# Attention with memory slots and a three-way maxout FFN: weights by column thirds, batch 1's sums in two parts, a new order of work

## The chip, the cores and the metric

The kernel runs on one core of one Trainium2 chip. The metric is the device time of a launch in microseconds (us), the median of several runs. A profile shows the same program from its first to its last instruction; that span is about 2 us shorter than the time. Work is spread over TensorE (matmul; PE in the profile), VectorE (DVE), ScalarE (ACT), GpSimd (POOL, here mostly the issuer of loads) and SyncE (SP, which issues the stores).

## The reference

Eight batches, eight heads, 576 positions, head size 64, and 32 memory slots per head; then a feed-forward block over all 4608 tokens of width 512, with an inner width of 768.

```python
a   = softmax(phi, axis=2)                      # [b, h, s, 32]
k_m = einsum('bhsm,bhsd->bhmd', a, k)           # 32 summed keys per head
v_m = einsum('bhsm,bhsd->bhmd', a, v)
attn = softmax(q @ k_m.T / sqrt(64), axis=-1)   # [b, h, s, 32]
x   = (attn @ v_m) rearranged to [4608, 512]
h   = maximum(maximum(x @ w1, x @ w2), x @ w3)  # [4608, 768]
out = h @ w_out                                 # [4608, 512], fp32
```

The kernel never forms `x`. It multiplies the summed values of a batch into the weights ("folds" them), so that the FFN works on the attention weights directly. It also uses max(a, b, c) = c + max(a - c, b - c, 0): w3 is subtracted from w1 and w2, and w3 @ w_out is computed once and folded too.

## The kernel before: the parts that matter

All matmul operands are bf16, sums are fp32 in PSUM. One pool of four PSUM buffers (two banks each) serves every matmul group.

```python
acc_pool = ctx.enter_context(tc.tile_pool(name="accp", bufs=4, space=bass.MemoryType.PSUM))
ctx.enter_context(tc.manual_schedule())         # engines keep the order of the text below
# loads; all but phi of batch 0 are issued by GpSimd, with a cast from fp32 to bf16 (phi: none)
load_ph(0); load_kv(0); load_q(0)               # load_kv(0): k and v in halves
load_w(2)                                       # w3, one transfer
nc.gpsimd.dma_start(out=wo_sb, in_=...)         # w_out
make_identity(nc, ident)
load_w(0); load_w(1)                            # w1, w2, one transfer each
load_ph(1); load_kv(1); load_q(1)               # load_kv: k, then v
# ... cut ...
EVAC = {"D": "avaa", "T": "vavav"}              # which engine drains: a ScalarE, v VectorE
```

Each step has a letter. `W@0` is the step W of batch 0.

```python
Z  warm_up(n)      n matmuls 128x512 on zeros (fill time on TensorE, results unused)
E  att_exp         e = exp(phi)                                   ScalarE
B  att_kv          72 small matmuls: e^T [k | v | 1] -> kvp       (the 1s give the sum of e)
N  att_kv_norm     1/sum, v part * 1/sum, k part * 1/sum          VectorE
K  att_kv_t        3 transposes of the normalised parts           VectorE drains
Q  att_q(n)        transpose of half of q                         VectorE
S  att_score       32 small matmuls, then two exps                ScalarE
M  att_sum(g)      sum over the slots by a matmul with ones
R  att_rec(g)      r = exp(-ln(sum)), two operations              ScalarE
X  att_mul(g)      attn = e2 * r                                  VectorE
W  w3_t(f2)        8 transposes of w3                             VectorE drains
O  w3_o(j)         6 matmuls: w3 @ w_out, a quarter               ScalarE drains
V  w_diff(n)       w1 - w3, w2 - w3, in three parts               VectorE
D  fold(b, n)      8 small matmuls 64x512; n = 3 folds w3 @ w_out; one PSUM buffer, drained to wp
F  ffn1(b, n)      4 matmuls 128x288; tile n // 2 of the inner width, n % 2 = 0 for w1, 1 for w2
T  ffn2(b, t)      6 + 2 matmuls 128x512, drained to SBUF and stored by SyncE
L  loads: L0 phi, L1 k and v, L2 q
```

```python
def w_diff(n):                                  # n-th 512 columns of [w1 | w2], 1536 wide
    c = n * BANK
    while c < (n + 1) * BANK:
        e = min((n + 1) * BANK, (c // DF + 1) * DF)
        nc.vector.tensor_tensor(out=w12[:, :, c:e], in0=w12[:, :, c:e],
                                in1=w_sb[:, :, 2, c % DF : c % DF + e - c], op=ALU.subtract)
        c = e

def ffn1(b, n):
    ft, w = n // 2, n % 2
    # ... lhsT = wps[b][:, g, w * DF + ft * P : w * DF + (ft + 1) * P] ...
    if w == 0:
        nc.scalar.activation(out=h1, in_=a, func=AF.Relu)                    # max(a - c, 0)
    else:
        nc.vector.tensor_tensor(out=hT[...], in0=a, in1=s["h1", ft], op=ALU.max)
```

The order of the first part, as it stands in the text of before:

```python
E@0 Z26@0 B@0 N@0 Z5@0 K@0 Q0@0 Q1@0 Z8@0 S@0 Z8@0 W1@0 W2@0 M0@0 W0@0 L0@2 R0@0
Z9@0 O2@0 M1@0 V0@0 X0@0 R1@0 O0@0 X1@0 V2@0 O3@0 L1@2 Z3@0 D0@0 O1@0 F6@0 F0@0 F2@0
D2@0 F4@0 V1@0 D3@0 D1@0 F7@0 F5@0 F10@0 F11@0 F1@0 E@1 F3@0 F8@0 F9@0 B@1 N@1 Q0@1
T3@0 K@1 Q1@1 T1@0 S@1 D1@1 L2@2 D0@1 M0@1 M1@1 R1@1 R0@1 X1@1 T0@0 X0@1 T2@0 E@2
...
```

A step's place in this text sets its place in each engine's own queue; across engines only the data, the buffers and the transfers hold it back.

Of the kernel before, what the change touches and what calls it, by code (L numbers as in the profile page):

```python
# [8 lines left out]
FP32 = mybir.dt.float32  # L9
BF16 = mybir.dt.bfloat16  # L10
AF = mybir.ActivationFunctionType
ALU = mybir.AluOpType
# [3 lines left out]
def kernel(  # L16
# [12 lines left out]
    nc = tc.nc  # L29
# [13 lines left out]
    BANK = 512  # L43

# [3 lines left out]
    quad = ctx.enter_context(tc.tile_pool(name="quad", bufs=4))  # L48
    opool = ctx.enter_context(tc.tile_pool(name="opool", bufs=6))
# [41 lines left out]
    def load_kv(b):  # L91
        kv = kvos[b % 2]
        loaded.setdefault(b, {})["kv"] = kv
        for h in halves if b == 0 else [slice(0, NP)]:
            for i, src in enumerate((k, v)):
                nc.gpsimd.dma_start(  # L96
                    out=kv[:, i].rearrange("p j c d -> p j (c d)")[:, h],
                    in_=by_pair(src, b)[:, h],
                )
# [8 lines left out]
    def load_w(i):  # L108
        w = (moe_w1, moe_w2, moe_w3)[i]
        nc.gpsimd.dma_start(  # L110
            out=w_sb[:, :, i], in_=w.rearrange("(j p) f -> p j f", p=P)
        )

    load_ph(0)
    load_kv(0)
    load_q(0)
    load_w(2)
    nc.gpsimd.dma_start(out=wo_sb, in_=moe_w_out.rearrange("(t p) c -> p t c", p=P))
    ident = const.tile([P, P], BF16, name="ident")
    make_identity(nc, ident)  # L120
    load_w(0)
    load_w(1)
    load_ph(1)
    load_kv(1)
    load_q(1)

# [18 lines left out]
    EVAC = {"D": "avaa", "T": "vavav"}  # L145

    def evacuate(kind, n, out_, in_):
        e = EVAC[kind][n]
        if e == "s":
            nc.scalar.copy(out=out_[:, 0], in_=in_[:, 0])  # L150
            nc.vector.tensor_copy(out=out_[:, 1], in_=in_[:, 1])
        elif e == "a":
            nc.scalar.copy(out=out_, in_=in_)  # L153
        else:
            nc.vector.tensor_copy(out=out_, in_=in_)  # L155


    def w3_t(f2):

        pt = acc_pool.tile([P, 2, NP, P], BF16, name="pt", tag="acc")  # L160
        for i in range(2):
            f = 2 * f2 + i
            for j in range(NP):
                nc.tensor.transpose(
                    pt[:, i, j, :], w_sb[:, j, 2, f * P : (f + 1) * P], ident
                )
        nc.vector.tensor_copy(out=w3T[:, 2 * f2 : 2 * f2 + 2], in_=pt)

    def w3_o(j):
        po = acc_pool.tile([P, DM], FP32, name="po", tag="acc")  # L170
        for f in range(FT):
            nc.tensor.matmul(
                po,
                lhsT=w3T[:, f, j, :],
                rhs=wo_sb[:, f, :],
                start=(f == 0),
                stop=(f == FT - 1),
            )
        nc.scalar.copy(out=w3o[:, j, :], in_=po)

    w12 = w_sb[:, :, 0:2].rearrange("p j i f -> p j (i f)")

    def w_diff(n):

        c = n * BANK
        while c < (n + 1) * BANK:
            e = min((n + 1) * BANK, (c // DF + 1) * DF)
            nc.vector.tensor_tensor(
                out=w12[:, :, c:e],
                in0=w12[:, :, c:e],  # L190
                in1=w_sb[:, :, 2, c % DF : c % DF + e - c],
                op=ALU.subtract,
            )
            c = e

# [9 lines left out]
    def att_kv(b, js=range(NP)):  # L207
        s = st[b]
        if "kvp" not in s:
            s["kvp"] = acc_pool.tile([P, NG, BANK], FP32, name="kvp", tag="acc")  # L210
        kv, kvp = loaded[b]["kv"], s["kvp"]
        for c in range(NC):
            for j in js:
                for a in range(NG):
                    r = slice(HP * a, HP * (a + 1))
                    nc.tensor.matmul(  # L216
                        kvp[M * j : M * (j + 1), a, 0 : 3 * D],
                        lhsT=s["e"][r, j, c, :],
                        rhs=kv[r, :, j, c, :],
                        start=(c == 0),  # L220
                        stop=(c == NC - 1),
                        tile_position=(HP * a, M * j),
                    )

    def att_kv_norm(b):

        s = st[b]
        kvp = s["kvp"]
        rden = work.tile([P, NG], FP32, name="rden")
        nc.vector.reciprocal(out=rden, in_=kvp[:, :, 2 * D])  # L230
        kvn = work.tile([P, 3, P], BF16, name="kvn")
        nc.vector.tensor_tensor(
            out=kvn[:, 0].rearrange("p (a d) -> p a d", a=NG),
            in0=kvp[:, :, D : 2 * D],
            in1=rden.unsqueeze(2).to_broadcast([P, NG, D]),
            op=ALU.mult,
        )
# [10 lines left out]
        s["kvn"] = kvn  # L248

    def att_kv_t(b):  # L250


        s = st[b]
        ps = acc_pool.tile([P, 3, P], BF16, name="kvtp", tag="acc")
        for n in range(3):
            nc.tensor.transpose(ps[:, n], s["kvn"][:, n], ident)  # L256
        kvt = work.tile([P, 3, P], BF16, name="kvt")
        nc.vector.tensor_copy(out=kvt, in_=ps)
        s["kvt"] = kvt
# [84 lines left out]
    def fold(b, n):  # L344
# [7 lines left out]
        for j in range(NP):  # L352
            for a in range(NG):
# [4 lines left out]
                    rhs=w12[r, j, n * BANK : (n + 1) * BANK] if n < 3 else w3o[r, j, :],  # L358
# [5 lines left out]
            "D", n, wp3s[b] if n == 3 else wps[b][:, :, n * BANK : (n + 1) * BANK], ps  # L364
# [5 lines left out]
    def ffn1(b, n):  # L370
# [4 lines left out]
        hT, attn = hts[b // 2], attns[b // 2]  # L375
        acc = acc_pool.tile([P, 2, BANK], FP32, name="acc", tag="acc")
        for g in range(NG):
            for h in range(2):
# [3 lines left out]
                    lhsT=wps[b][:, g, w * DF + ft * P : w * DF + (ft + 1) * P],  # L382
# [5 lines left out]
        if w == 0:  # L388
            h1 = s["h1", ft] = quad.tile([P, 2, SH], BF16, name="h1")
            nc.scalar.activation(out=h1, in_=a, func=AF.Relu)  # L390
# [10 lines left out]
    def ffn2(b, t, last=False):  # L401
# [4 lines left out]
        if last:  # L406
            return ffn2_last(b, c0)
# [31 lines left out]
        evacuate("T", t, ot, po)  # L439
# [34 lines left out]
    def first_kv():  # L474
        for n, h in enumerate(halves):
            att_kv(0, range(NP)[h])
            if n == 0:
                warm_up(9)


    def issue(b, n):

        if not 0 <= b < B or (n == "T4" and b % 2 == 0):
            return
        i = int(n[1:]) if len(n) > 1 else None
        {
            "L": lambda: (load_ph, load_kv, load_q)[i](b),
            "E": lambda: [att_exp(b, h) for h in (halves if b == 0 else [slice(0, NP)])],
            "B": lambda: att_kv(b) if b else first_kv(),
            "N": lambda: att_kv_norm(b),  # L490
            "K": lambda: att_kv_t(b),
# [5 lines left out]
            "D": lambda: fold(b, i),  # L497
            "F": lambda: ffn1(b, i),
            "T": lambda: ffn2(b, i),
            "W": lambda: w3_t(i),  # L500
            "O": lambda: w3_o(i),
# [4 lines left out]
    def run(b, text):  # L506

        for w in text.split():
            issue(b + w.count("+") - w.count("-"), w.rstrip("+-"))

    for w in """
        E@0 Z26@0 B@0 N@0 Z5@0 K@0 Q0@0 Q1@0 Z8@0 S@0 Z8@0 W1@0 W2@0 M0@0 W0@0 L0@2 R0@0
        Z9@0 O2@0 M1@0 V0@0 X0@0 R1@0 O0@0 X1@0 V2@0 O3@0 L1@2 Z3@0 D0@0 O1@0 F6@0 F0@0 F2@0
        D2@0 F4@0 V1@0 D3@0 D1@0 F7@0 F5@0 F10@0 F11@0 F1@0 E@1 F3@0 F8@0 F9@0 B@1 N@1 Q0@1
        T3@0 K@1 Q1@1 T1@0 S@1 D1@1 L2@2 D0@1 M0@1 M1@1 R1@1 R0@1 X1@1 T0@0 X0@1 T2@0 E@2
        D3@1 F2@1 F0@1 F3@1 D2@1 B@2 N@2 F1@1 Q1@2 F8@1 Q0@2 L0@3 F6@1 F4@1 L1@3 F10@1 K@2
        F7@1 F5@1 L2@3 S@2 F11@1 D2@2 F9@1 E@3 M0@2 T2@1 M1@2 R0@2 R1@2 X0@2 L0@4 T0@1 D0@2
        X1@2 D3@2 B@3 N@3 D1@2 L1@4 T1@1 F2@2 F6@2 Q1@3 F3@2 E@4 K@3 F8@2 L2@4 F7@2 L0@6
        Q0@3 F4@2 F10@2 F5@2 F0@2 S@3 L0@5 T4@1 M1@3 F11@2 R1@3 F1@2 M0@3 R0@3 X0@3 T3@1
        F9@2 D2@3 D1@3 L2@5 X1@3 B@4 D0@3 T1@2 F8@3 L1@5 N@4 F2@3 K@4 F9@3 Q1@4 F10@3 F0@3  # L520
        E@5 F3@3 Q0@4 F4@3 T3@2 S@4 F5@3 F1@3 L1@6 T0@2 F6@3 M0@4 M1@4 F11@3 R0@4 T2@2 R1@4
        F7@3 D3@3 B@5 D3@4 Q0@5 Q1@5 D2@4 L2@6 N@5 X1@4 T0@3 L1@7 X0@4 K@5 T1@3 L2@7 D0@4
        D1@4 E@6 L0@7
    """.split():
        n, b = w.split("@")
        issue(int(b), n)
    for b in range(4, B - 1):
        run(b, "L0+++++ D1+ T4- S+ T3- F6 F2 F0 F4 F7 F3 Q0++ F8 F10 F1 M1+ F11 F9 Q1++")
        run(b, "M0+ R1+ R0+ X1+ F5 T2- D0+ B++ D3+ L2++++ D2+ T1 L1++++ N++ K++ E+++ X0+")
        run(b, "T0")  # L530
    run(B - 1, "F4 F6 F2 F0 F5 T2- F8 F7 F1 F3 F9 F10 T4- F11 T3- T4 T1 T2 T0")
    ffn2(B - 1, 3, last=True)


# [28 lines left out]
```

The softmax here doesn't subtract the row's maximum and nothing guards it: scores larger than these inputs give would overflow.

## Time and profile before

| | |
|---|---|
| time, median of 3 | 171.32 us (170.85 to 171.52) |
| span of the profile | 169.3 us |
| TensorE busy | 161.3 us (95%) |
| VectorE busy | 98.9 us (58%) |
| ScalarE busy | 101.3 us (60%) |
| GpSimd busy | 28.4 us (17%) |
| granted TensorE clock | 1.000 |
| moved by DMA | 31.76 MB, mean 188 GB/s |
| HBM read and written | 39.32 MB and 9.44 MB |

The busy share of TensorE includes warm-up matmuls, 65 of them in the profile, all in the first 27 us. A matmul's busy time runs from its start to its modelled end, and matmuls overlap; the time from one start to the next is what it costs in a row of them. "Moved" counts the bytes as they arrive, so a load with a cast from fp32 counts half of what it reads.

The stages follow the order above. Up to about 28.9 us the attention of batch 0 and the work on w3 wait for loads. Then ffn1 of batch 0 begins, and at 37.7 us the sums of batch 1. From there the attention of a batch runs between the ffn1 and ffn2 of the batches ahead of it.

### The profile page before, as it was taken

What the parts mean: (1) busy time and instruction counts of PE and PEld (TensorE: products, weight loads), DVE (VectorE), ACT (ScalarE), POOL (GpSimd) and SP (SyncE); (2) the same over time, 40 slices, a digit from 0 to 9 for tenths busy, and PEclk for the clock granted to TensorE, in tenths of its full rate; (3) what the DMA queues carried; (4) which work ended last, traced back from release to release, by engine and by line L of the source; (5) the groups of instructions that cost most, each with busy time, mean ns of one, the idle gap of its engine ahead of it and who ended that gap; (6) DMA issues with size and microseconds to landing.
All of it is one profiled execution on the core that took longest, in us unless ns stands there. A gap on an engine that the chain in (4) does not pass through costs nothing.

```text
span 169.3 us, 4498 instructions
## 1 busy us (share of the span) xinstructions
PE 161.3 (95%) x1927; PEld 91.1 (54%) x1948; DVE 98.9 (58%) x164; ACT 101.3 (60%) x150; POOL 28.4 (17%) x43
## 2 busy tenths in 40 slices
PE   7999999889999999999999999999999999999991
PEld 2454544464457557566565447645854475566350
DVE  6406406896379687477667845944794439238130
ACT  4100536951997988686858578787874387752200
POOL 7951111113114101503102400000000000000000
PEclk9999999999999999999999999999999999999999
DMA  5999999999999999999999999952103310221333
GB/s 156 164 205 210 207 210 271 216 211 275 234 278 288 208 281 259 233 328 283 233 228 239 235 259 248 251 192 99 54 4 124 124 66 4 109 80 62 121 127 126
DMA packets 21973, 31.76 MB, mean 188 GB/s; under 512 B 1216, under 2 KB 16576, under 8 KB 21952
## 3 DMA queue, kind: packets, MB, share of 16 engines
q0 software_dynamic: 16080, 21.43, 65.8%
q1 hardware_dynamic: 5728, 9.90, 16.7%
q8 instruction: 15, 0.25, 0.6%
q10 hardware_dynamic: 144, 0.13, 0.2%
q14 instruction: 6, 0.05, 0.1%
HBM read 39.32 MB, written 9.44 MB: 288 GB/s over the span
## 4 chain that ended last, share of the span: by engine, by line
PE 74%; DMA 20%; issue 1%; POOL 1%; ACT 1%; POOLq 0%
PE po L410 27%; PE acc L380 25%; DMA kvo<-in_v_dram 20%; PE po L419 8%; PE wps L355 4%; PE kvp L216 3%; PE sm L311 2%; PE sc L290 1%; POOL kvo L96 1%; PE po L428 1%; PE po L451 1%; PE kvtp L256 1%; ACT e L299 1%; ACT ot L153 0%; PE po L459 0%
## 5 line engine op out<-in xcount | busy, mean ns | idle before, releaser
L380 PE MATMUL acc<-attn,wp 128*128 128x288 bf16 x384 | 52.0, 286 | 0.3 <-ACT wp L153 0.3
L410 PE MATMUL po<-wo_sb,hT 128*128 128x512 bf16 x192 | 50.0, 379 | 1.1 <-issue 0.2
L392 DVE TENSOR_TENSOR hT<-acc,h 128x576 bf16<-128x576 f32 x48 | 34.5, 751 | 19.7 <-PE acc L380 17.8
L380 PEld LDWEIGHTS <-wp 128*128 128x128 bf16 x384 | 36.8, 98 | 13.1 <-issue 1.1
L390 ACT ACTIVATE h<-acc 128x576 bf16<-128x576 f32 x48 | 28.6, 654 | 11.3 <-PE acc L380 11.3
L410 PEld LDWEIGHTS <-hT 128*128 128x128 bf16 x210 | 19.4, 97 | 22.2 <-issue 3.7
L153 ACT CAST wp<-wps 128x1024 bf16<-128x1024 f32 x24 | 23.6, 1016 | 5.4 <-PE wps L355 5.3
L155 DVE COPY ot<-po 128x512 f32<-128x512 f32 x20 | 13.8, 688 | 17.8 <-PE po L419 12.5
L299 ACT ACTIVATE e<-sc 128x576 bf16<-128x576 f32 x16 | 9.5, 650 | 17.7 <-PE sc L290 17.7
L140 PE MATMUL po<-warm 128*128 128x512 bf16 x65 | 17.7, 420 | 1.5 <-DVE warm L128 1.2
L419 PE MATMUL po<-wp,attn 128*128 128x512 bf16 x62 | 18.4, 379 | 0.0
L153 ACT COPY ot<-po 128x512 f32<-128x512 f32 x15 | 8.8, 588 | 16.0 <-PE po L419 16.0
L335 DVE TENSOR_TENSOR attn<-e,r 128x576 bf16<-128x576 bf16 x16 | 11.9, 747 | 2.7 <-ACT r L330 2.7
L268 DVE STREAM_TRANSPOSE qT<-qq 128x576 f32<-128x576 f32 x16 | 12.0, 762 | 0.8 <-DMA qq<-in_q_dram 0.8
L324 ACT ACTIVATE ln<-sm 128x576 f32<-128x576 f32 x16 | 10.3, 646 | 3.1 <-PE sm L311 3.1
L140 PEld LDWEIGHTS <-warm 128*128 128x128 bf16 x68 | 6.8, 106 | 10.0 <-issue 3.5
L330 ACT ACTIVATE r<-ln 128x576 f32<-128x576 f32 x16 | 10.9, 683 | 0.5
L155 DVE CAST wp<-wps 128x1024 bf16<-128x1024 f32 x8 | 9.7, 1218 | 2.1 <-PE wps L355 2.1
L205 ACT ACTIVATE e<-ph 128x1152 bf16<-128x1152 f32 (+1 forms) x9 | 9.5, 1058 | 2.0 <-DMA ph<-in_phi_dram 1.9
L96 POOL DMA_DIRECT2D kvo<-in_k_dram x9 | 6.8, 750 | 20.7 <-PE wps L355 13.0
L419 PEld LDWEIGHTS <-attn 128*128 128x128 bf16 x62 | 6.1, 98 | 7.3
L89 POOL DMA_DIRECT2D ph<-in_phi_dram x7 | 5.3, 760 | 26.6 <-ACT e L205 22.6
(46 smaller groups left out, 111.8 us busy)
## 6 DMA issues: line engine op xcount, KB each, us to landing
out_dram<-ot SPq DMA_DIRECT2D x35, 256.0 KB, 3.9
qq<-in_q_dram POOLq DMA_DIRECT2D x8, 576.0 KB, 19.6
ph<-in_phi_dram POOLq DMA_DIRECT2D x7, 576.0 KB, 18.5
kvo<-in_k_dram POOLq DMA_DIRECT2D x7, 576.0 KB, 17.5
kvo<-in_v_dram POOLq DMA_DIRECT2D x7, 576.0 KB, 20.3
w_sb<-in_moe_w_dram POOLq DMA_DIRECT2D x3, 768.0 KB, 18.9
wo_sb<-in_moe_w_out_dram POOLq DMA_DIRECT2D x1, 768.0 KB, 16.5
ph<-in_phi_dram SPq DMA_DIRECT2D x2, 288.0 KB, 2.9
```

The lines of the kernel that those rows point to most:

```text
L140: nc.tensor.matmul(po[:, 0:BANK], lhsT=warm[:, 0:P], rhs=warm, start=True, stop=True)
L153: nc.scalar.copy(out=out_, in_=in_)
L155: nc.vector.tensor_copy(out=out_, in_=in_)
L268: nc.vector.transpose(out=s["qT"][:, j].rearrange("p j c r e -> p (j c r e)").bitcast(FP32), in_=loaded[b]["q"][:, j].rearrange("p j c d - ...
L299: nc.scalar.activation(out=e2[:, a].rearrange("p (t r c) -> p t r c", t=2, c=NC), in_=sc[a][:, :, 0:SH].rearrange("p t (c r) -> p t r c", ...
L330: nc.scalar.activation(out=r, in_=ln, func=AF.Exp, scale=-1.0)
L335: nc.vector.tensor_tensor(out=attns[b // 2][:, g, (b % 2) * S : (b % 2 + 1) * S], in0=s["e2"][:, g, 0:S], in1=s["r", g], op=ALU.mult,)
L380: nc.tensor.matmul(acc[:, h, 0:SH], lhsT=wps[b][:, g, w * DF + ft * P : w * DF + (ft + 1) * P], rhs=attn[:, g, c0 : c0 + SH], start=(g == ...
L390: nc.scalar.activation(out=h1, in_=a, func=AF.Relu)
L392: nc.vector.tensor_tensor(out=hT[:, ft, (b % 2) * S : (b % 2 + 1) * S].rearrange("p (h n) -> p h n", h=2), in0=a, in1=s["h1", ft], op=ALU.max,
L410: nc.tensor.matmul(po, lhsT=hT[:, fc, c0 : c0 + P], rhs=wo_sb[:, fc, :], start=(fc == 0), stop=False,)
L419: nc.tensor.matmul(po, lhsT=attn[:, g, c0 : c0 + P], rhs=wp3s[b][:, g, :], start=False, stop=(g == NG - 1),)
```

## The change

It does four things.

- **Thirds.** w1 and w2 are loaded in three column thirds of 256 each, alternating (w1 third 0, w2 third 0, w1 third 1, ...). The difference and the fold of a third take the 256 columns of w1 and of w2 together. One fold therefore holds both halves of two tiles of the inner width, and ffn1 on those tiles may begin when the first third is there.
- **Batch 1 in parts.** k is summed and transposed first (`B0 N0 K0`), and v later (`B1 N1 K1`), with the load of q ahead of the load of v. The scores need k and q only.
- **Drains one by one.** Every drain of a PSUM buffer has a default engine, and `!` behind a step takes the other one.
- **A new order** for the whole kernel. All loads have a place in it; relu results have a pool of six buffers of their own (four, shared with another tile, before).

k and v of batch 0 are loaded whole, v first. The diff, cut to its core:

```diff
+    hpool = ctx.enter_context(tc.tile_pool(name="hpool", bufs=6))
...
-    def load_kv(b):
-        ...
-        for h in halves if b == 0 else [slice(0, NP)]:
-            for i, src in enumerate((k, v)):
+    def load_kv(b, i):
+        kv = loaded.setdefault(b, {})["kv"] = kvos[b % 2]
+        nc.gpsimd.dma_start(
+            out=kv[:, i].rearrange("p j c d -> p j (c d)"), in_=by_pair((k, v)[i], b)
+        )
...
-    def load_w(i):
+    def load_w(i, n=None):
+        c = slice(0, DF) if n is None else slice(n * W3, (n + 1) * W3)
         w = (moe_w1, moe_w2, moe_w3)[i]
         nc.gpsimd.dma_start(
-            out=w_sb[:, :, i], in_=w.rearrange("(j p) f -> p j f", p=P)
+            out=w_sb[:, :, i, c], in_=w.rearrange("(j p) f -> p j f", p=P)[:, :, c]
         )
...
-    EVAC = {"D": "avaa", "T": "vavav"}
+    EVAC = {"D": "avaa", "T": "vavav", "K": "v", "W": "vvv", "O": "aaaa", "F": "aaaaaa"}
+    def evacuate(kind, n, swap, out_, in_, relu=False):
+        if (EVAC[kind][n] == "a") != swap:
+            ... ScalarE: relu or copy ...
+        elif relu:
+            nc.vector.tensor_scalar_max(out=out_, in0=in_, scalar1=0.0)
...
     def w_diff(n):
+        c = slice(n * W3, (n + 1) * W3)
+        for i in range(2):
             nc.vector.tensor_tensor(
+                out=w_sb[:, :, i, c], in0=w_sb[:, :, i, c], in1=w_sb[:, :, 2, c],
                 op=ALU.subtract,
             )
...
+    def att_kv(b, part=None):
+        cols = {None: slice(0, 3), 0: slice(0, 3, 2), 1: slice(1, 2)}[part]
+        nd = {None: 3 * D, 0: 2 * D, 1: D}[part]
...
-                    rhs=w12[r, j, n * BANK : (n + 1) * BANK] if n < 3 else w3o[r, j, :],
+                    rhs=w_sb[r, j, 0:2, n * W3 : (n + 1) * W3] if n < 3 else w3o[r, j, :],
...
+        f0 = (ft // 2) * BANK + w * W3 + (ft % 2) * P
-                    lhsT=wps[b][:, g, w * DF + ft * P : w * DF + (ft + 1) * P],
+                    lhsT=wps[b][:, g, f0 : f0 + P],
```

The new order, its first part and the stretch around batch 3 and its end (`Y2` and `Y3` load w3 and w_out, `H0` to `H2` the thirds of w1, `H3` to `H5` those of w2, `I` makes the identity; `L0` phi, `L1` k, `L2` v, `L3` q):

```python
L2@0 L1@0 E@0 Z48@0 B@0 N@0 L3@0 I@0 Z4@0 K@0 Q0@0 Q1@0 Z8@0 S@0 Z3@0 M0@0 R0@0 M1@0
R1@0 Y2@0 W0@0 X0@0 W1@0 Y3@0 H0@0 W2@0 Z10@0 O3@0 H3@0 H1@0 H4@0 H2@0 H5@0 X1@0 V0@0
O2@0 O0@0 D0@0 O1@0 V1@0 D1@0! V2@0 F2@0 F0@0 L0@1 F3@0 L1@1 F6@0 F1@0 D2@0 F7@0 E@1
F4@0! F5@0 F10@0 F8@0 F11@0 F9@0 B0@1 N0@1 D3@0 T3@0 L3@1 Q0@1 Q1@1 K0@1! T2@0! S@1
L2@1 B1@1 M0@1 L1@2 N1@1 R0@1 K1@1 X0@1 M1@1 L0@2 R1@1 T1@0 D1@1 L2@2 D2@1 E@2 T0@0!
... cut ...
B@4 N@4 R0@3 X0@3 D1@3! D0@3 T3@2 Q0@4 L3@5 K@4 F6@3 Q1@4 F4@3 Q1@5 D2@3 D3@3 T2@2!
F10@3 S@4 F11@3 F0@3 F8@3 ...
... cut ...
F11@7 F2@7 F9@7 F4@7 F3@7 F5@7 T1@6 T2@6! T3@6 T0@7! T0@6! T1@7 T2@7! T0@4! T0@5! T2@5!
T4@7! T3@7
```

## The prediction

> **What bounds the kernel now.** I read the page's busy slices first, then the chain of waits in order of time, then TensorE's waits, and last the timeline of the first 50 us.
>
> The busy slices of the page (tenths of 4.2 us each):
>
> ```profile
> PE   7999999889999999999999999999999999999991
> ...
> DVE  6406406896379687477667845944794439238130
> ACT  4100536951997988686858578787874387752200
> PEclk9999999999999999999999999999999999999999
> DMA  5999999999999999999999999952103310221333
> ```
>
> TensorE is busy throughout, but the first ten slices contain 65 warm-up matmuls, so this row cannot tell useful work from filling. DMA is full for 27 slices.
>
> The chain of waits, in order of time (start us, us, what):
>
> ```profile
> 11.66 25.91 DMA kvo<-in_v_dram
> 37.70 0.94 PE kvp L216 x72
> ...
> 48.41 1.58 PE acc L380 x12
> ...
> 143.04 0.77 PE wps L355 x24
> ...
> 155.04 1.29 PE po L410 x6
> ```
>
> Until 37.6 us a transfer ends last: v of batch 1. From 37.70 on nearly everything is TensorE. TensorE's waits agree:
>
> ```profile
> PE kvp L216 <- DMA kvo<-in_v_dram: 0.5, 1, 0.5
> PE wps L355 <- DVE w_sb L188: 0.4, 1, 0.4
> ```
>
> The useful work follows from the chain's steps. An ffn1 call (4 matmuls) is 0.49 us, an ffn2 call 1.29 + 0.43 = 1.72, a fold (8) 0.34, a kv sum (72) 0.74, a score 0.41, an att_sum 0.25, a kv transpose 0.19; by the six-matmul ffn2 step a w3_o is 1.29; a w3_t is about 0.51 (0.064 per start on the timeline). So 96 x 0.49 + 36 x 1.72 + 32 x 0.34 + 8 x (0.74 + 0.41 + 2 x 0.25 + 0.19) + 4 x 1.29 + 3 x 0.51, plus about 0.5 for the split ffn2 calls, is about 141.7 us. Before 37.70 there is one kv sum, transpose, score and two att_sums (1.84), three w3_t (1.53), four w3_o (5.16), four folds (1.36) and twelve ffn1 (5.88): 15.8. That leaves 125.9 of work for the 128.0 us from 37.70 to the last matmul's end near 165.7. **After 37.7 only about 2.1 us can be gained by any order; the rest lies before it.**
>
> The timeline of that first part (start, us, engine, line, operation, idle before and releaser):
>
> ```profile
> 14.49 0.74 POOL L104 DMA_DIRECT2D qq<-in_q_dram  x1 [2.09 <-DMA qq<-in_q_dram]
> ...
> 19.00 0.76 POOL L89 DMA_DIRECT2D ph<-in_phi_dram  x1 [3.76 <-DMA w_sb<-in_moe_w_dram]
> ...
> 22.35 1.46 PE L172 MATMUL po<-wo_sb,w3T 128*128 128x512 bf16 x6 [0.16 <-DMA wo_sb<-in_moe_w_out_dram]
> 22.74 0.74 POOL L96 DMA_DIRECT2D kvo<-in_k_dram  x1 [2.99 <-DMA wo_sb<-in_moe_w_out_dram]
> ...
> 26.06 1.23 DVE L188 TENSOR_TENSOR w_sb<-w_sb 128x2048 bf16<-128x2048 bf16 x1 [5.03 <-DMA w_sb<-in_moe_w_dram]
> ...
> 28.99 1.63 PE L380 MATMUL acc<-attn,wp 128*128 128x288 bf16 x12
> ...
> 29.78 2.43 DVE L188 TENSOR_TENSOR w_sb<-w_sb 128x2048 bf16<-128x2048 bf16 x3 [1.15 <-DMA w_sb<-in_moe_w_dram]
> ```
>
> GpSimd's issues wait for earlier transfers, so their starts mark landings: q about 14.2, w3 18.4, w_out 22.2, w1 26.0, w2 29.8. A weight matrix (1.57 MB of fp32) takes 3.8 us, 413 GB/s; a k or v (1.18 MB) 2.8. The completion events put phi, k, v, q of batch 1 at 32.0, 34.7, 37.6 and 40.5.
>
> **What the skill says.** The Trainium skill, "Trainium Kernel Development and Optimization", Performance Expectations, calls matmul busy time a bad measure because matmuls are pipelined; this trace agrees (an ffn1 matmul is shown as 286 ns and starts 0.122 us apart), so I count starts. "DMA: Bandwidth & Descriptors", Specifications, puts line rate at pieces of 512 B and up and the fabric's ceiling at 435 GB/s: the 413 agrees, but no load here has 512 B rows, which a third of a weight (256 bf16) has. "TensorE: Matmul & The Clock Gate", Part 1, says that TensorE starts at half clock and doubles after some 3.4 us: here warm-up starts are 0.43 us apart until 5.78 us, then 0.21. "TensorEngine Tiling (Array Packing)", Key Properties, says that a change of tiling mode drains the engine: here the first full-size matmul after a fold loses about 0.28 us. Both orders have about the same number of changes, 49 and 50, so nothing is gained there.
>
> **Part by part.**
>
> *Thirds.* A third needs 3.8 / 3 = 1.27 us if rows of 512 B are as good, and the order alternates w1 and w2. Landings: 23.5, 24.7 (first pair), 26.0, 27.3 (second), 28.5, 29.8 (third). Each difference is two 1024-element operations of 0.68: V0 is done at 26.5, V1 at 29.1, V2 at 31.6. Before, both halves of any h were possible only after 29.8. Now the first third could start ffn1 at about 28.
>
> *But the new order does not start there.* Its head is 48 warm-ups. From 1.2 us, about eleven cold ones reach 5.78 and 37 x 0.213 = 7.9 more end at 13.7, while k and v land near 11.4 as before. Before, the second half of the kv sum started at 12.01. From then the steps repeat those of before, 1.7 us later: reciprocal 14.75, transposes 15.7, scores 17.8 (16.0 before), exp of the scores to 19.6, att_sums 19.1 and 19.75, w3_t from 20.0 (now behind both att_sums) to 21.7, ten warm-ups (2.1) to 23.9. So w3_o starts at about 24.0 (22.35 before). Three w3_o and the first fold end at 28.3, the fourth w3_o at 29.9, and fold D1 stands ahead of the first ffn1: that starts near 30.5 (28.99 before). The fold ahead (0.34) and the last w3_o are then already done.
>
> *To batch 1.* From 30.5 the twelve ffn1 and fold D2 are 6.2 us. ScalarE has w3_o, D1, two relus, a third relu, D2, the exp of batch 1 and two relus in that time (0.6 + 1.0 + 1.8 + 1.0 + 1.16 + 1.2), which with four PSUM buffers costs some 0.4. The k sum of batch 1 starts at about 37.2, where k (34.7) no longer stops it: 0.5 sooner than 37.70, with the fold of w3o still to come. Then the k sum, that fold, two ffn2 and the transpose lead to the scores at about 42.4 (42.29 before), with the same batch 0 work done, but the v sum still to do: 0.74 more, with two mode changes of 0.2 to 0.3. The q transposes (two of 0.77, after q at 37.6) are ready at about 40.4. So loading k and q first hides waits that the filling work covers anyway, and the second sum is extra. **Start: +1.2 us.**
>
> *Drains.* The page's groups (busy, mean ns, idle before):
>
> ```profile
> L390 ACT ACTIVATE h<-acc 128x576 bf16<-128x576 f32 x48 | 28.6, 654 | 11.3 <-PE acc L380 11.3
> L153 ACT CAST wp<-wps 128x1024 bf16<-128x1024 f32 x24 | 23.6, 1016 | 5.4 <-PE wps L355 5.3
> L155 DVE COPY ot<-po 128x512 f32<-128x512 f32 x20 | 13.8, 688 | 17.8 <-PE po L419 12.5
> L153 ACT COPY ot<-po 128x512 f32<-128x512 f32 x15 | 8.8, 588 | 16.0 <-PE po L419 16.0
> ```
>
> Counted with the marks, 31 folds (24 before) and 34 ffn2 (16) drain on ScalarE. That is 7 x 1.0 + 18 x 0.59 = 17.6 us more: 101.3 becomes 119, VectorE's 98.9 about 78. Over the whole that fits under TensorE, but not in every stretch. From R0 to F8 of batch 3 in the new order, TensorE has four folds, two ffn2, six ffn1, one score, one transpose: 8.3 us; ScalarE has R 1.33, four folds 3.9, two ffn2 1.2, five relus 3.0, one score 1.2: 10.6. The densest stretch of that length before is 1.14 to 1, and no wait of TensorE shows there. Four PSUM buffers absorb part of an excess of 2.3; I estimate 0.2 to 0.4 lost in each of three or four such stretches. **+0.8.** Against it, the new order ends in ffn2 calls that wait for nothing late, and hpool's six buffers hold back fewer relus: of the 2.1 us above I give **-0.9**.
>
> Sum: 169.3 + 1.2 + 0.8 - 0.9 = 170.4 of span, and with the 2.0 us between span and time before, 172.4.
>
> **Rivals.** *The thirds bring what they promise*: warm-ups end sooner (the clock rises earlier), ffn1 starts at 29, batch 1 at 35. Then 2 us less at the start, 0.9 back for the second sum: about 170. For it: the weights do land late and k early. Against it: D1 ahead of the first ffn1. *512 B rows are slow*: at 1.6 us a third the last lands at 31.8 and everything behind it 2 us later: 174. For it: shorter packets; against it: transfers with rows of 1024 (w_out), 1152 (k) and 1536 B (w1) all take time in proportion to their bytes (3.8, 2.8, 3.8 us). *ScalarE becomes the bound* in the middle: every stretch pays its 2 us, 176 or more. Against it: 119 is well below 142.
>
> **Range and chances.** The steps scatter by about 1 us at the start, 1.5 in the middle: 169.4 to 175.2. Faster by 2% (under 167.9) needs more than all slack after 37.7: 0.07. Slower by 2% (over 174.7) needs slow thirds or ScalarE stretches: 0.12. Within: 0.81.
>
> **What would show it.** Right: first w3_o near 24, first ffn1 near 30.5, k sum of batch 1 near 37 without a DMA wait, last third near 29.8, ScalarE busy 119, small TensorE idle before folds and ffn1 after ScalarE. Wrong: ffn1 near 28.5, thirds landing after 31, or more than 2 us of TensorE idle after 45.

## The result and the profile after

| | before | after |
|---|---|---|
| time, median | 171.2 us | 172.15 us (171.71 to 172.38) |
| ratio to before, 95% interval | | 1.0056 (1.0034 to 1.0078) |
| span of the profile | 169.3 | 170.2 |
| VectorE / ScalarE busy | 98.9 / 101.3 | 81.6 / 117.3 |

The changed kernel is about 1 us slower. A second measurement of the same kernel beside later runs, on another chip, gave 171.89 where the kernel before had 171.02, and a ratio of 1.0069 (1.0048 to 1.009).

The busy slices of the changed kernel's page, in tenths of 4.26 us each:

```profile
PE   7999998999999999989999999999999999999991
...
DVE  6404374793457606887376576447483027300000
ACT  4100636875987998889999998997898876242420
...
PEclk9999999999999999999999999999999999999998
DMA  5999999999999999999999999931101321043433
```

ScalarE is the fuller of the two helpers now, at nine tenths through the middle, and VectorE has nothing to do at the end. DMA is full for as long as before, some 110 us.

Its chain of waits (start us, us, what), the head and the one place in the middle where it leaves the engines:

```profile
1.19 12.62 PE po L135 x48
13.81 0.92 PE kvp L208 x72
...
23.61 3.88 PE po L168 x18
...
30.27 2.56 PE acc L378 x20
...
36.70 0.73 PE kvp L208 x72
...
41.34 0.41 PE sc L287 x23
...
48.02 2.94 PE acc L378 x24
...
59.80 18.24 DMA qq<-in_q_dram
...
81.53 20.85 DMA kvo<-in_v_dram
102.52 0.94 PE kvp L208 x72
```

Before, the chain left the DMA queue at 37.6 us for good. Now its head is TensorE's own warm-ups, so v of batch 1 no longer counts, but between 59.8 and 102.4 us the chain runs over transfers: q of batch 4, then v of batch 6, issued at 81.53 and needed at 102.52. This view follows whatever was released last, and those 42 us are not lost time; but it says which events had no slack.

TensorE's waits of the changed kernel, without the first 1.2 us and two of 0.2 ("issue" is time in which the engine waited for nothing that the profile shows):

```profile
PE wps L352 <- ACT w3o L148: 0.6, 1, 0.6
PE kvp L208 <- DVE attn L332: 0.5, 1, 0.5
PE kvp L208 <- issue: 0.4, 1, 0.4
PE kvp L208 <- DMA kvo<-in_v_dram: 0.3, 1, 0.3
```

Three of these four stand at a kv sum (L208): the 0.4 at the v sum of batch 1, the 0.5 at batch 4, the 0.3 at batch 6. (The 0.6 is fold D1, for which VectorE's difference ended at 29.80 us and a copy on ScalarE at 29.85.) The timeline of TensorE at batches 4 and 6:

```profile
74.28 0.53 PE L378 MATMUL acc<-attn,wp 128*128 128x288 bf16 x3
75.32 0.94 PE L208 MATMUL kvp<-kvo,e 64*32 64x192 bf16 x72 [0.51 <-DVE attn L332]
...
101.57 0.63 PE L352 MATMUL wps<-w_sb,kvt 64*32 64x512 bf16 x16
102.52 0.94 PE L208 MATMUL kvp<-kvo,e 64*32 64x192 bf16 x72 [0.32 <-DMA kvo<-in_v_dram]
```

At 75.32 an unrelated multiply on VectorE is named, which ended at the same moment, but the completion events, which tell when each of the 16 parts of a load is there, put the last part of v of batch 4 at 75.2. In five profiles of this order and its variants below the sum waits there, and each time it starts 0.1 us behind that landing: 75.2 and 75.32, 76.0 and 76.09, 76.1 and 76.19, 74.9 and 74.99, 74.7 and 74.85. So the wait is put down to v. The landings of v against the start of the sum that uses them, in us:

| batch | before: landing, sum | after: landing, sum |
|---|---|---|
| 2 | 48.99, 50.15 | 49.90, 51.11 |
| 3 | 60.25, 61.20 | 63.48, 64.76 |
| 4 | 72.46, 75.36 | 75.19, 75.32 |
| 5 | 89.41, 90.75 | 91.21, 92.05 |
| 6 | 96.80, 109.09 | 102.38, 102.52 |
| 7 | 109.10, 125.21 | 113.16, 117.49 |

v is not the only late load. In the profile of the second measurement, an ffn1 also waits for a drain that VectorE makes for batch 3:

```profile
PE acc L378 <- DVE kvt L152: 0.4, 1, 0.4
```

This drain of the kv transpose stands behind a transpose of q of batch 3 in VectorE's queue, and that q landed at 68.80 (68.06 in the first profile, without a wait of TensorE).

Where the time went shows best at points where both kernels have the same work behind them. From the timeline and the counts:

| | before | after |
|---|---|---|
| first w3_o / first ffn1 of batch 0 | 22.35 / 28.99 | 23.45 / 30.20 |
| first k (or kv) sum of batch 1 | 37.70 | 36.63 |
| scores of batch 1 | 42.29 | 41.27 |
| first ffn1 of batch 1, with two folds behind it | 48.03 | 47.85 |
| from there to the last matmul's start | 117.35 | 118.31 |

(In the kernel before, a third fold of 0.34 lies ahead of that ffn1, which starts at 48.37; it is taken off in one row and added in the next.) At 48 us the changed kernel is **0.2 us ahead**. It loses **1.0 us after that**, with the same work left.

### The profile page after: what moved, and what is told of

It reads as the page before. It is cut to its first block, busy times and chain, and to the rows that moved or that the text cites. A ratio compares the mean times of both kernels' runs of the same rounds, so it can differ in the third digit from the quotient of the medians.

```text
span 170.2 us, 4678 instructions
## 1 busy us (share of the span) xinstructions
PE 162.8 (96%) x2025; PEld 91.0 (53%) x2025; DVE 81.6 (48%) x141; ACT 117.3 (69%) x176; POOL 29.9 (18%) x45
## 4 chain that ended last, share of the span: by engine, by line
PE 68%; DMA 23%; DVE 3%; issue 2%; ACT 1%; POOL 1%; POOLq 0%; ACTq 0%; DVEq 0%
PE po L408 20%; PE acc L378 18%; DMA kvo<-in_v_dram 12%; DMA qq<-in_q_dram 11%; PE po L135 10%; PE po L417 6%; PE po L168 3%; PE kvp L208 3%; PE wps L352 3%; PE sm L308 1%; PE sc L287 1%; PE po L426 1%; PE po L449 1%; DVE hT L390 1%; PE pt L160 1%
## 5 line engine op out<-in xcount | busy, mean ns | idle before, releaser
L408 PE MATMUL po<-wo_sb,hT 128*128 128x512 bf16 x210 | 51.2, 380 | 0.2 <-DVE hT L390 0.2
L390 DVE TENSOR_TENSOR hT<-acc,h 128x576 bf16<-128x576 f32 x48 | 35.2, 754 | 27.0 <-PE acc L378 25.6
L148 ACT COPY ot<-po 128x512 f32<-128x512 f32 x33 | 19.4, 589 | 19.3 <-PE po L417 17.2
L148 ACT CAST wp<-wps 128x1024 bf16<-128x1024 f32 x31 | 29.9, 1021 | 3.3 <-PE wps L352 3.3
L135 PE MATMUL po<-warm 128*128 128x512 bf16 x73 | 18.7, 413 | 1.2 <-DVE warm L123 1.2
L135 PEld LDWEIGHTS <-warm 128*128 128x128 bf16 x73 | 7.3, 104 | 10.6 <-issue 3.0
L104 POOL DMA_DIRECT2D qq<-in_q_dram x8 | 6.0, 749 | 27.1 <-DVE qT L265 26.5
L208 PE MATMUL kvp<-kvo,e 64*32 64x192 bf16 (+2 forms) x648 | 8.2, 235 | 1.2 <-DVE attn L332 0.5
```

Of the source, the lines that this page charges most:

```text
L135: nc.tensor.matmul(po[:, 0:BANK], lhsT=warm[:, 0:P], rhs=warm, start=True, stop=True)
L208: nc.tensor.matmul(kvp[M * j : M * (j + 1), a, 0:nd], lhsT=s["e"][r, j, c, :], rhs=kv[r, cols, j, c, :], start=(c == 0), stop=(c == NC - 1 ...
L390: nc.vector.tensor_tensor(out=hT[:, ft, (b % 2) * S : (b % 2 + 1) * S].rearrange("p (h n) -> p h n", h=2), in0=a, in1=s["h1", ft], op=ALU.max,
L408: nc.tensor.matmul(po, lhsT=hT[:, fc, c0 : c0 + P], rhs=wo_sb[:, fc, :], start=(fc == 0), stop=False,)
```

## The experiments

Theory A: this 1 us is lost because loads of the middle land too late for the new order. Theory B: it is lost to ScalarE, which now drains nearly everything. Beside these two, the start was taken apart. Each run stands beside the kernel before on the same chip, and the ratios are to that; the chips differ by some tenths (the kernel before had 170.95 to 171.37). "Changed" below is the repeat, 171.89.

### Drains back on their default engines

```diff
-        if (EVAC[kind][n] == "a") != swap:
+        if EVAC[kind][n] == "a":
```

> The changed kernel with every drain on its default engine: no step is swapped, so one fold in four and three ffn2 drains in five go back to VectorE, as in the kernel before. Theory A (the loss of the middle is two waits on v of batches 4 and 6; drains cost nothing): 172.1 +- 0.4, ScalarE busy near 101 us, the kv sums of batches 4 and 6 still wait for v. Theory B (the loss is ScalarE's load, 117 us busy): 171.2 or less, and the two kv sums start about 0.5 us sooner because ScalarE frees PSUM earlier.

178.95 us, ratio 1.0433 (1.04 to 1.0465): 6 to 7 us slower than the changed kernel, which neither theory expected. ScalarE is at 102.1 us, VectorE at 100.4, both far from full. The first loss is at 48 us; timeline of this run, TensorE and VectorE only:

```profile
48.15 0.41 PE L378 MATMUL acc<-attn,wp 128*128 128x288 bf16 x2
48.34 0.69 DVE L152 COPY ot<-po 128x512 f32<-128x512 f32 x1 [0.79 <-PE po L417]
48.95 0.75 DVE L332 TENSOR_TENSOR attn<-e,r 128x576 bf16<-128x576 bf16 x1
49.75 0.53 PE L378 MATMUL acc<-attn,wp 128*128 128x288 bf16 x3 [1.20 <-DVE attn L332]
```

The same place in the changed kernel (weight loads left out):

```profile
47.18 0.75 DVE L332 TENSOR_TENSOR attn<-e,r 128x576 bf16<-128x576 bf16 x1
47.20 1.18 ACT L194 ACTIVATE e<-ph 128x1152 bf16<-128x1152 f32 x1
47.42 0.59 PE L417 MATMUL po<-wp,attn 128*128 128x512 bf16 x2
47.85 2.37 PE L378 MATMUL acc<-attn,wp 128*128 128x288 bf16 x18
48.27 0.59 ACT L148 COPY ot<-po 128x512 f32<-128x512 f32 x1
```

The text of the order is `T0@0! X1@1 F4@1`. With the swap, ScalarE drains T0 and VectorE has made the attention of batch 1 (X1) before T0's last matmul ends. Without it, the copy of T0 stands ahead of X1 in VectorE's queue. It cannot start until TensorE has finished T0, X1 waits behind it, and the next ffn1 waits 1.2 us for X1. A drain's engine is a place in a queue, not only a load. Of the 6.5 us that TensorE waits from there on, 5.7 are put down to VectorE; only this first place is followed up here. Theory B in its simple form falls: with 15 us less on ScalarE the kernel is slower. That ScalarE costs nothing at all is not shown by this run, since placement hides it.

### The kv sums of batches 4 and 6 later

```diff
-B@4 N@4 R0@3 X0@3 D1@3! D0@3 T3@2
+R0@3 X0@3 D1@3! D0@3 B@4 N@4 T3@2
-D1@5! D2@5 B@6 X0@5 D0@5 T0@3!
+D1@5! D2@5 X0@5 D0@5 B@6 T0@3!
```

> The changed kernel with the kv sums of batches 4 and 6 placed behind two folds and one fold of the batch before, so that about 0.8 and 0.5 us of TensorE work covers the wait for v. Nothing else moves. Theory A (waits on v): 171.2, between 170.8 and 171.6, and no wait on v before either sum. Theory B (ScalarE's load): 172.1, the folds now wait for their PSUM buffers in place of the sums.

172.46, ratio 1.0058 (1.0039 to 1.0078): no gain, where theory A had 170.8 to 171.6. In the profile v of batch 4 landed at 75.6, and its sum, at 76.1, did not wait. But the sum of batch 5 now stood 0.1 us behind its v (92.61 and 92.74), and that of batch 6 still did (103.4 and 103.5). The slowest part of the weights was 3.5 us behind the fastest here, against 2.2 to 2.7 in the changed kernel's profile, and everything came later. The run moved a wait on but did not bring the loads nearer, so it doesn't decide.

### Without 18 stores, in both kernels

```diff
-        nc.sync.dma_start(out=rows, in_=ot)
+        if b >= 4:
+            nc.sync.dma_start(out=rows, in_=ot)
```

The rows of batches 0 to 3 are computed and drained but not stored, so the outputs lack them.

> The changed kernel as it is, to stand beside the other runs of this group. 172.15 was measured; every theory expects 171.7 to 172.6, 0.3 to 0.9 us over the kernel before. Its kv sums of batches 4 and 6 start within 0.2 us of the landing of v, unless its loads land sooner in this execution.

> The changed kernel without the stores of the ffn2 results of batches 0 to 3 (18 stores of 256 KB; their rows of the output are left out; all else is done). Theory A (loads of the middle land too late because DMA is full, and stores that now come earlier push them back): v of batches 4 and 6 lands 3 us or more sooner, no sum waits, and the time falls by 0.8 to 1.3, to 171.0 or less. Rival C (the waits on v hide nothing: other engines are as late): less than 0.4 us fall although v lands sooner.

> The kernel before without the stores of the ffn2 results of batches 0 to 3 (18 stores; their rows of the output are left out). It is the control of the same cut in the changed kernel, which took 1.3 us off. If the changed order is the one that runs too close to its loads, the kernel before loses less: 0 to 0.5 us. If stores cost both orders the same: 1.0 to 1.5.

| | with stores | without 18 | gain |
|---|---|---|---|
| changed | 171.89, 1.0069 (1.0048 to 1.009) | 170.59, 0.9971 (0.9954 to 0.9987) | 1.30 |
| before | 170.95 | 170.41, 0.997 (0.9956 to 0.9985) | 0.54 |

Without those stores the two kernels have the same time. In the changed one, v of batch 4 lands at 68.7 and of batch 6 at 93.5, against 76.0 and 102.4, and the sums start when TensorE is free. Timeline of TensorE in that run:

```profile
74.24 0.65 PE L378 MATMUL acc<-attn,wp 128*128 128x288 bf16 x4
74.83 0.94 PE L208 MATMUL kvp<-kvo,e 64*32 64x192 bf16 x72
...
101.07 0.62 PE L352 MATMUL wps<-w_sb,kvt 64*32 64x512 bf16 x16
101.57 0.94 PE L208 MATMUL kvp<-kvo,e 64*32 64x192 bf16 x72
```

No idle time stands in brackets. From the first ffn1 of batch 1 to the last matmul it takes 117.1 us, and the kernel before without stores, with its third fold added, 117.35: the 1.0 us of the table above is gone. ScalarE's drains are all still there (117.2 us busy). So theory A holds for the middle, and the new order with its drains costs TensorE nothing once the loads are in time.

### The first ffn1 ahead of the second fold

```diff
-O1@0 V1@0 D1@0! V2@0 F2@0 F0@0 L0@1 F3@0
+O1@0 V1@0 F2@0 F0@0 D1@0! V2@0 L0@1 F3@0
```

> The changed kernel with the first two ffn1 of batch 0 ahead of fold D1, which waited 0.6 us for the difference of the second third. If the start passes on to the end: 0.4 to 0.7 us less than the changed kernel, first ffn1 at 29.2 in place of 30.2. If the loads that land later (k at 35.8, q 38.6, v 41.5, and those of the middle) set the pace: no difference, within 0.2, and TensorE waits for them instead.

172.53, ratio 1.0091 (1.0072 to 1.0111). The first ffn1 started at 29.05, 1.1 us sooner than in the changed kernel, but the first ffn1 of batch 1 at 48.21, later than 47.85: fold D1 now drains later, and TensorE waited 0.76 us for it at 31.9. Then v of batch 4 landed at 76.1. Here the gain at the first ffn1 was worth nothing by itself.

### Halves, a later sum, fewer warm-ups

```diff
+        for h in halves if b == 0 else [slice(0, NP)]:
             nc.gpsimd.dma_start(
-                out=kv[:, i].rearrange("p j c d -> p j (c d)"), in_=by_pair((k, v)[i], b)
+                out=kv[:, i].rearrange("p j c d -> p j (c d)")[:, h],
+                in_=by_pair((k, v)[i], b)[:, h],
             )
```

> The changed kernel with k and v of batch 0 loaded in halves, as before (v, v, k, k). In the kernel before, the slowest of the 16 parts of a load came 1.1 to 1.4 us behind the fastest up to the weights, in the changed kernel 2.2 to 3.5. If whole first loads cause that lag: lag under 1.5 again, all weights 0.8 to 1 us sooner, time 0.5 to 1 us under the changed kernel. If it comes from elsewhere: lag over 2 and the time within 0.3.

171.55, ratio 1.0032 (1.0008 to 1.0056), 0.34 under the changed kernel; the two intervals overlap, so the gain is not clear of noise. The slowest part of a load ran 1.3 to 2.0 us behind the fastest up to the weights (2.2 to 2.7 in the changed kernel's first profile; the 3.5 of the expectation is the run with the later sums), v of batch 4 landed at 74.1 and its sum at 74.7 did not wait. The wait at batch 6 stayed (landing 101.9, start 102.04).

The next run adds to it:

```diff
-D1@5! D2@5 B@6 X0@5 D0@5 T0@3! M1@5 R1@5 N@6 K@6 L3@7 ... T4@3! X1@5 S@6 T2@3!
+D1@5! D2@5 X0@5 D0@5 T0@3! B@6 M1@5 R1@5 N@6 L3@7 ... T4@3! K@6 X1@5 T2@3! S@6
```

> The changed kernel with k and v of batch 0 in halves, and the kv sum of batch 6 behind one fold and one ffn2 (2.1 us of TensorE work), its transposes and the scores of batch 5 to 6 moved behind one ffn2 each. With halves alone: 171.55, a wait of 0.7 us on v of batch 6 left, none on batch 4. Theory A: that wait goes, 0.4 to 0.7 less, 170.9 to 171.2. If other work waits in its place: 171.5.

172.16, ratio 1.0067 (1.0049 to 1.0085). Batch 6 no longer waited for v, but the ffn2 put ahead of it waited 0.3 us for its own input, an att_sum 0.2, and v of batch 4 landed at 74.9 this time, with its wait of 0.5 back. Then, on top, `Z48@0` became `Z41@0`:

> The kernel with halves and the later sum of batch 6, and with 41 warm-ups in place of 48 at the head (1.5 us). The prediction held that the warm-ups push the start: then the first w3_o starts near 22.8 and 0.5 to 1 us are gained over the run with 48. If the second third of w1 and w2 sets when ffn1 of batch 0 starts (30.2 in two executions whose warm-ups ended 0.7 us apart): no change, within 0.3, first ffn1 still at 29.5 to 30.3.

171.81, ratio 1.0055 (1.0035 to 1.0076); the two intervals overlap. The first w3_o started at 22.29, the first ffn1 at 29.20, the first ffn1 of batch 1 at 47.0, 0.66 us sooner than in the run before it (47.66). But the kv sum of batch 4 stands at 74.85 against 74.99, right behind v's landing at 74.7. The timeline of TensorE:

```profile
73.77 0.53 PE L380 MATMUL acc<-attn,wp 128*128 128x288 bf16 x3
74.85 0.94 PE L210 MATMUL kvp<-kvo,e 64*32 64x192 bf16 x72 [0.55 <-DVE attn L334]
```

So the warm-ups do set the start of w3_o, as the prediction had it (1.5 us sooner here). Of that 0.6 us reach the first ffn1, since fold D1 now waits 0.8 us for a difference, and at batch 4 the loads have taken nearly all of it back.

### One sum for batch 1

```diff
-F9@0 B0@1 N0@1 D3@0 T3@0 L3@1 Q0@1 Q1@1 K0@1! T2@0! S@1 L2@1 B1@1 M0@1 L1@2 N1@1 R0@1 K1@1 X0@1 M1@1 L0@2 R1@1 T1@0
+F9@0 L2@1 D3@0 T3@0 B@1 N@1 L3@1 T2@0! K@1! Q0@1 Q1@1 T1@0 S@1 M0@1 L1@2 R0@1 X0@1 M1@1 L0@2 R1@1
```

> The changed kernel with batch 1's k and v summed in one pass: loads k, v, q; sum, normalise and transpose whole; the sum stands behind the first ffn2 of batch 0, and one more ffn2 stands ahead of the scores to cover q. Theory A (the second sum costs 0.7 to 0.8 us of TensorE and its lead covers nothing that filling work does not): between 171.3 and 172.1. Rival (k and q ahead of v bring the 1.0 us by which the scores of batch 1 came sooner): 173, with TensorE idle over 1 us ahead of batch 1's scores or sums of e.

172.87, ratio 1.0085 (1.006 to 1.0111). The interval overlaps that of the changed kernel, so the time alone does not tell the two apart. In the profile the sum stood at 39.16, behind v; the scores at 43.75 (41.27 changed); the first ffn1 of batch 1 at 48.83 (47.85), and 0.4 of that 1.0 is there already at the first w3_o. TensorE waited 0.8 us between the scores and the sums of e, where the changed kernel does the v sum and its transpose:

```profile
45.04 0.95 PE L308 MATMUL sm<-e,blkones 128*128 128x288 bf16 x4 [0.81 <-ACT e L296]
```

So the work that the split adds fills a wait here, and no cost of it shows. One ffn2 had to move with it, so any difference belongs to the pair.

### The thirds, and whole first loads in the kernel before

```diff
-            "H": lambda: load_w(i // 3, i % 3),
+            "H": lambda: load_w(i // 3) if i % 3 == 0 else None,
```

> The changed kernel with w1 and w2 loaded whole, one after the other, at the places of their first thirds; differences and folds still by thirds. If loading by thirds is what lets the first fold (27.4 us) and ffn1 (30.2 us) of batch 0 start: the first difference ends near 31.5, the first ffn1 starts at 32.5 to 33, and the time is 173.5 to 175. If other work (w3_o, the warm-ups) sets the start anyway: within 0.5 of 172.15. The six thirds took 8.3 us against 7.6 for two whole weights, so the loads behind them would land about 0.4 us sooner.

176.28, ratio 1.0269 (1.0221 to 1.0317); by the two ratios that is some 3.4 us over the changed kernel. The page's clock row and the waits and timeline of TensorE:

```profile
PEclk9999999569999999999999999999999999999999
```

```profile
PE wps L352 <- DVE w_sb L181: 4.2, 1, 4.2
```

```profile
32.00 0.63 PE L352 MATMUL wps<-w_sb,kvt 64*32 64x512 bf16 x8 [4.17 <-DVE w_sb L181]
32.56 2.74 PE L168 MATMUL po<-wo_sb,w3T 128*128 128x512 bf16 x6
...
35.79 1.62 PE L378 MATMUL acc<-attn,wp 128*128 128x288 bf16 x6
```

The first fold waits for the whole of both weights: it is at 32.00, not 27.43, 4.6 us late. After 4.2 us of idling the granted clock is at about half, and the six matmuls of a w3_o take 2.74 us in place of 1.47. From the fold to the first ffn1 it takes 3.79 us in place of 2.77, so the first ffn1 is at 35.79, 5.6 us late; some 2.5 was expected.

This run also bears on theory A. From its first ffn1 of batch 1, at 54.27, to the last matmul it takes 117.1 us, as in the run without stores. So late, the order no longer runs into its loads: v of batch 4 landed 1.8 us ahead of its sum, v of batch 6 1.9.

The last run changes the kernel before:

```diff
-        for h in halves if b == 0 else [slice(0, NP)]:
-            for i, src in enumerate((k, v)):
+        for h in [slice(0, NP)]:
+            for i, src in ((1, v), (0, k)) if b == 0 else enumerate((k, v)):
```

> The kernel before with one thing of the change: k and v of batch 0 loaded whole, v first. If whole first loads cause the lag of the slowest part (2.0 to 2.8 us with whole loads, 1.0 to 1.9 with halves): lag over 2 from the first load to the weights, all later loads 0.5 to 1 us later, and 0.3 to 0.6 us more than the kernel before, with a longer wait for v of batch 1. If the lag is a matter of the execution: lag under 1.7, no difference.

175.84, ratio 1.027 (1.0242 to 1.0297), for a reason that was not expected. The lag was 1.7 to 2.2 us, between the two expectations, and the weights landed 0.6 us later. But the 26 warm-ups ended long before k was there. The waits and the clock row of the page:

```profile
PE kvp L216 <- DMA kvo<-in_k_dram: 3.8, 1, 3.8
```

```profile
PEclk9985899999999999999999999999999999999999
```

The eight matmuls between the two half sums, in the kernel before and in this run:

```profile
10.19 1.89 PE L140 MATMUL po<-warm 128*128 128x512 bf16 x8 [0.16 <-issue]
```

```profile
14.53 3.62 PE L140 MATMUL po<-warm 128*128 128x512 bf16 x8 [0.33 <-issue]
```

With 3.8 us of waiting the clock falls, these eight take 3.62 us in place of 1.89, and the first w3_o comes at 28.07, not 22.35. The Trainium skill, "TensorE: Matmul & The Clock Gate", Part 1, says that the clock goes back to half after an idle window of some 3.4 us; waits of 3.8 and 4.2 us here agree, and none of the other profiles, whose waits are under 1.3 us, shows such a slice. The 48 warm-ups of the changed kernel bridge such a wait: they reach to 13.7 us, past the landing of k at 12.81. Over all runs the lag of the slowest part up to the weights was 1.5 to 3.6 us with whole first loads and 0.6 to 2.1 with halves; the ranges overlap, and why a part lags stays open.

## Why the prediction was right, point by point

The time, 172.15, is 0.25 from the predicted 172.4, and the span came out at 170.2 for 170.4: +0.9 us where the three terms add up to +1.1. **None of the three terms held. Their errors cancelled, and that the number is so close is luck.**

- **Thirds.** "A third needs 1.27 us", landings 23.5 to 29.8. The completion events give 24.5, 25.9, 27.2, 29.1, 30.2 and 31.5: a start 1.0 late with w_out (23.2), then 8.3 us for six, 1.38 each. So rows of 512 B are close to the rate of long ones here, as the Trainium skill, "DMA: Bandwidth & Descriptors", Specifications, says; the slow-rows rival (1.6) falls. The last landing is past 31, which the prediction had named as a sign of being wrong; over half of its 1.7 us come from the loads ahead. The prediction put no figure on what the thirds are worth: in this order, whose first fold needs both weights, whole loads cost some 3.4 us. The kernel before folds from w1 alone first, and has its first ffn1 at 28.99 with whole loads.
- **The head.** Step by step it held: kv sum 13.74 (13.7), scores 17.77 (17.8), w3_o 23.45 (24.0), first ffn1 30.20 (30.5), k sum 36.63 (37.2) with no DMA wait. One step was hidden: k landed at 12.81, not "near 11.4", and only the long warm-ups kept that from counting.
- **"Start: +1.2 us"** failed: it is -0.2. The scores of batch 1 came at 41.27, not "about 42.4". Two terms were mis-sized. From the first ffn1 to the scores it took 11.1 us for 11.9: the twelve ffn1 and the fold 6.43 for 6.7, of which 0.4 had been put on ScalarE's backlog, and the k sum, fold, two ffn2 and transpose 4.64 for 5.2, where their bare costs add up to 4.71. And "the second sum is extra" left out that it fills the 0.8 us in which the exps of the scores run: the one-sum run waited that long.
- **"Drains: +0.8"** failed as a cause. ScalarE is busy 117.3 (119 predicted) and VectorE 81.6 (78). But from 48 to 115 us ScalarE was busy 62 of 67 us without a TensorE wait that it explains, and without 18 stores the order runs as well as the old one. Four buffers do absorb it.
- **"-0.9" of slack recovered** did not come: the middle lost 1.0 instead. What cost it is in no rival: the loads. The waits view of the kernel before has no transfer of the middle in it, but the landings against the uses of every batch were the thing to list: there, v of batch 4 had 3 us to spare and v of batch 6 12, which this change used up.
- **Why the loads are later.** DMA is full in both kernels until 110 us. In the changed one v of batch 4 lands at 75.2 (72.5 before) and of batch 6 at 102.4 (96.8). Of the first 2.7 us, 1.0 is already there at phi of batch 1 (33.0 for 32.0). By the landing of v of batch 4 nine stores had been issued, the last at 68.2; before it was eight, the eighth only 0.5 us ahead of the landing. One to two stores of 256 KB are 0.6 to 1.3 us, worked out from 413 GB/s; the rest is not accounted for. Of the 5.6 us at batch 6, the other 2.9 are about one load: the new order has q of batch 6 ahead of its k and v (`L3@6 ... L1@6 L2@6`), where the kernel before loads it behind them, and a load of that size takes 2.8 us. No run moved that load alone. At the same time the order wants batch 6 sooner, after about 79 us of useful TensorE work in place of 86 (by the prediction's costs).
- **Readings** that were off without moving the sum: the DMA row is full for 25 slices, not 27; the traces show 52 and 51 changes of tiling mode, not 49 and 50; and in them the next full-size matmul mostly starts 0.31 to 0.34 us behind a fold's last start, from which no loss of 0.28 can be read.

## What to carry to other kernels

When TensorE and DMA are both full, reorder only with the table of landings against uses beside you: a reordering that saves time ahead of a late load gives it back there, and one that issues stores earlier, or puts another load ahead, makes the load later. An engine assigned to a drain is a place in that engine's queue, and what stands behind it waits for the drain's producer. Warm-up matmuls that look like waste may be what keeps the clock up across a wait; change the loads and their number must follow.

## What was not expected of the hardware

- A wait of TensorE of 3.8 or 4.2 us cost twice: the wait, and then matmuls at about half clock (3.62 us for eight that otherwise took 1.89).
- The 16 parts of one of GpSimd's loads up to the weights end 0.6 to 3.6 us apart, from the first load on. The lag differs between executions of nearly the same program (2.2 and 3.5 us at w_out), and with it the landings of the loads behind (23.2 and 24.3 us for w_out).
- Two kernels that differ only in the engine of 28 drains lay 6 to 7 us apart, with neither engine full in either (ScalarE 117.3 and 102.1 us busy, VectorE 81.6 and 100.4).
